# The first 640 steps of a banded-attention and feed-forward kernel, put into another explicit order

## The chip, the cores and the metric

The kernel runs on one core of a Trainium2 chip. Five engines work side by side, each through its own instruction list in order: TensorE (PE, matmuls; PEld is its weight load), VectorE (DVE), ScalarE (ACT), GpSimd (POOL) and SyncE (SP); SP, ACT and POOL also issue DMAs. The metric is the device time of one execution in microseconds, the median of three runs. [...]

## The reference

Attention with a causal window of 64 over q, k, v of shape (8, 8, 576, 64) in float32, then a feed-forward layer over the 4608 tokens of width 512:

```
scores = scale * q @ k.T                  # kept where 0 <= i - j < 64, else -1e9
attn   = softmax(scores)                  # minus the row's maximum, exp, divided by the sum
x      = (attn @ v) as (4608, 512)
h      = x @ w_in                         # (512, 2048), given as float64
out    = maximum(0.01 * h, h) @ w_out     # (2048, 512), given as float64
```

## The kernel before

The tokens are cut into 9 chunks of 512 columns. Three chunks go through an "early" feed-forward path, the other six through a later one with seven products in place of eight (line 1243 and line 1309 of the profile). Attention goes in pairs m of two query units (128 queries); each pair has two blocks b = 2m and 2m+1 of four heads. Every product is made from a high and a low float32 part (three matmuls per product), so each weight and each activation has to be split on DVE and ACT first. The float64 weights come as 32 raw tiles n (even: w_in, odd: w_out, tile f = n // 2) and are turned into float32 on DVE with integer operations.

The first stage, which this change is about, is written step by step in a string ORDER. A step's name is a kind and a number:

- attention: `S` scores of pair m on PE (64 small matmuls, L369, with two mask matmuls, L403, ahead of them but for m = 0); `Z` masks of the first pair; `E` copies a block's scores to memory (blocks 0 and 1 on DVE, L413, the others on ACT, L415); `P` the maximum over partitions on POOL (L423); `N` subtracts that maximum in PSUM by a matmul (blocks 0 to 3, L437), `sub` does so on DVE (L428, later blocks); `exp` on ACT; `V` the product with v on PE (L458); `sm`, `rec`, `y` the normalisation on DVE (L465, L470, L477); `T` a transpose on PE (L484); `H` and `L` the high part on ACT (L488) and low part on DVE (L492) of x.
- weights: `raw` the DMA of 512 KB (three buffers), `bits`, `sign`, `clamp`, `join` on DVE (L317, L321, L329, L334), `abs` on ACT between sign and clamp (L325), `chi` the high part on ACT and a DMA of the float32 tile to DRAM (`w_single`, L337 and L338), `rest` the low part on DVE (L342). `join` of tile n needs the tile that n-2 has sent off.
- feed-forward: `M` is x times w_in of job k (12 matmuls, L522), `lk`, `gh` (ACT) and `gl` (DVE, L536) the activation, `W` the product with w_out (L558). Jobs 0 to 5 are half chunks. M of job k needs the `rest` of its w_in tile and the `L` of the chunk's pairs.
- `X` with a number n is n matmuls without use (L594), `idle` in the trace.

After these 514 steps come 2303 planned operations whose order stands as numbers in a second table, PLACES (`arrange`, L442). They hold the rest of the weights, the stores of split weights, the other attention pairs and everything behind. At the end the kernel pins each engine to the order in which its instructions were written, so the tables alone set each engine's list. Nothing is reordered between engines at run time: an engine waits at the head of its list. SP's list holds the loads of q, k and v and the first three raw tiles; ACT's list holds the other raw loads.

Of the kernel before, what the change touches and what calls it, by code (L numbers as in the profile page):

```python
# [61 lines left out]
PLACES = """  # L62
# [134 lines left out]
def band_attention_ffn(ctx: ExitStack, tc: tile.TileContext, qk, vW, vL, w_in, w_out, eye_mask, out, outT):  # L197
# [415 lines left out]
    def step(name):  # L613
        kind = name.rstrip("0123456789")
        return partial(acts[kind], int(name[len(kind) :]))

    order, late = ORDER.split("|")
    for name in order.split():
        step(name)()
    prev = jobs[-1]  # L620


    plan = []

# [951 lines left out]
```

## Time and profile before

| | |
|---|---|
| median of 3 runs | 841.18 us (840.93 to 842.61) |
| span of the profiled execution | 841.2 us |
| PE busy | 829.1 us, 99% |
| DVE busy | 630.8 us, 75% |
| ACT busy | 369.7 us, 44% |
| POOL busy | 381.5 us, 45% |
| granted TensorE clock, mean | 0.998 of full |

The profiled execution's span equals the median, so sums made in the span can be set against the median directly. The first stage fills roughly the first 90 us. An engine's share of busy time is a mean over stages; in the first stage DVE is nearly as full as PE.

### The profile page before, as it was taken

What the parts mean: (1) busy time and instruction counts of PE and PEld (TensorE: products, weight loads), DVE (VectorE), ACT (ScalarE), POOL (GpSimd) and SP (SyncE); (2) the same over time, 40 slices, a digit from 0 to 9 for tenths busy, and PEclk for the clock granted to TensorE, in tenths of its full rate; (3) what the DMA queues carried; (4) which work ended last, traced back from release to release, by engine and by line L of the source; (5) the groups of instructions that cost most, each with busy time, mean ns of one, the idle gap of its engine ahead of it and who ended that gap; (6) DMA issues with size and microseconds to landing.
All of it is one profiled execution on the core that took longest, in us unless ns stands there. A gap on an engine that the chain in (4) does not pass through costs nothing.

```text
span 841.2 us, 16743 instructions
## 1 busy us (share of the span) xinstructions
PE 829.1 (99%) x6733; PEld 678.1 (81%) x6733; DVE 630.8 (75%) x912; ACT 369.7 (44%) x599; POOL 381.5 (45%) x216
## 2 busy tenths in 40 slices
PE   8999999999999999989999999999999999999997
PEld 5777888888888888868888888887888888888886
DVE  6999897777766698667888987559799863366773
ACT  4666555344423355243564442233545422325432
POOL 5332000897867747687672116797941111111110
PEclk9999999999999999999999999999999999999999
DMA  9886866987887899999999798899998996677772
GB/s 327 278 276 209 310 223 225 319 287 259 277 295 251 271 342 379 365 299 359 361 321 308 224 316 251 255 282 241 261 278 243 317 257 184 190 197 200 212 200 89
DMA packets 131005, 225.75 MB, mean 268 GB/s; under 512 B 15856, under 2 KB 53744, under 8 KB 130928
## 3 DMA queue, kind: packets, MB, share of 16 engines
q0 software_dynamic: 53568, 88.09, 38.8%
q10 hardware_dynamic: 36608, 78.26, 27.6%
q1 hardware_dynamic: 40752, 58.34, 21.7%
q8 instruction: 53, 0.87, 0.4%
q14 instruction: 24, 0.20, 0.1%
HBM read 167.28 MB, written 57.26 MB: 267 GB/s over the span
## 4 chain that ended last, share of the span: by engine, by line
PE 89%; DMA 5%; DVE 3%; issue 1%; ACT 1%; POOL 0%; DVEq 0%; ACTq 0%
PE z L1309 27%; PE m L1243 25%; PE acc L1047 11%; PE h L1038 11%; PE acc L558 4%; PE s L369 4%; PE h L522 4%; PE o L829 3%; DMA w_sums<-pspare 2%; DMA qk<-qk 1%; DMA raw<-w_in 1%; DMA raw<-w_out 1%; DMA w_single<-w 1%; PE o L458 0%; DVE raw L321 0%
## 5 line engine op out<-in xcount | busy, mean ns | idle before, releaser
L1243 PE MATMUL m<-pfew,p 128*128 128x512 f32 x720 | 171.6, 394 | 3.0 <-ACT pxa L1249 2.5
L1243 PEld LDWEIGHTS m<-pfew,p 128*128 128x128 f32 x720 | 135.5, 189 | 32.5 <-ACT pxa L1249 2.9
L1309 PE MATMUL z<-gs,p 128*128 128x512 f32 (+1 forms) x360 | 86.0, 387 | 0.0
L1047 PE MATMUL acc<-p,gs 128*128 128x512 f32 x324 | 80.7, 393 | 0.0
L1309 PE MATMUL z<-pxa,p 128*128 128x512 f32 x324 | 78.5, 391 | 0.0
L1309 PEld LDWEIGHTS z<-gs,p 128*128 128x128 f32 x360 | 67.3, 188 | 13.9
L1309 PE MATMUL z<-pspare,p 128*128 128x512 f32 x324 | 78.0, 389 | 0.0
L1252 DVE TENSOR_TENSOR pxa<-m,pxa 128x512 f32<-128x512 f32 x60 | 41.2, 688 | 48.5 <-PE m L1243 43.6
L770 POOL PARTITION_ALL_REDUCE g<-late_f x20 | 36.3, 1842 | 86.6 <-DVE late_f L755 71.5
L1227 POOL DMA_DIRECT2D p<-w_first x42 | 31.7, 755 | 93.7 <-PE m L1243 51.6
L1309 PEld LDWEIGHTS z<-pspare,p 128*128 128x128 f32 x324 | 60.7, 188 | 12.6
L1309 PEld LDWEIGHTS z<-pxa,p 128*128 128x128 f32 x324 | 60.5, 188 | 12.9 <-issue 0.2
L1243 PE MATMUL m<-pxb,p 128*128 128x512 f32 x288 | 70.6, 391 | 0.0
L1047 PEld LDWEIGHTS acc<-p,gs 128*128 128x128 f32 x324 | 60.0, 188 | 12.8
L773 POOL PARTITION_ALL_REDUCE late_o<-late_f x20 | 65.2, 3274 | 9.6 <-ACT late_f L781 7.4
L773 POOL PARTITION_ALL_REDUCE late_o<-e x18 | 61.5, 3432 | 16.6 <-issue 7.9
L1252 DVE TENSOR_TENSOR p<-m,pxa 128x512 f32<-128x512 f32 x60 | 40.7, 687 | 36.6 <-PE m L1243 35.9
L773 POOL PARTITION_ALL_REDUCE late_o<-late_e x18 | 59.3, 3321 | 10.6 <-ACT late_e L781 6.0
L1243 PEld LDWEIGHTS m<-pxb,p 128*128 128x128 f32 x288 | 53.8, 188 | 11.4
L1227 POOL DMA_DIRECT2D p<-w_sums x24 | 18.0, 749 | 93.1 <-PE z L1309 76.8
L1038 PE MATMUL h<-pxa,p 128*128 128x512 f32 x228 | 55.9, 392 | 0.0
L1038 PEld LDWEIGHTS h<-pxa,p 128*128 128x128 f32 x228 | 42.4, 188 | 9.0
(201 smaller groups left out, 1600.5 us busy)
## 6 DMA issues: line engine op xcount, KB each, us to landing
p<-w_first POOLq DMA_DIRECT2D x42, 1024.0 KB, 7.0
p<-w_sums POOLq DMA_DIRECT2D x24, 1024.0 KB, 6.7
p<-w_second POOLq DMA_DIRECT2D x18, 1024.0 KB, 6.9
qk<-qk ACTq DMA_DIRECT2D x26, 512.0 KB, 6.2
w_single<-w ACTq DMA_DIRECT2D x32, 256.0 KB, 3.7
raw<-w_out ACTq DMA_DIRECT2D x15, 512.0 KB, 4.5
raw<-w_in ACTq DMA_DIRECT2D x14, 512.0 KB, 4.3
more_v<-vL ACTq DMA_DIRECT2D x14, 512.0 KB, 6.0
```

What stands on the lines that cost most here:

```text
L369: nc.tensor.matmul(ps[j][t, c : c + QB], k[i][s, p], q[s, w, p], start=not begun and (not more or (w, p) == (0, 0)), stop=not begun and no ...
L522: nc.tensor.matmul(ps, a[:, k, :], b[:, k, part], start=n == 0, stop=n == len(terms) - 1)
L558: nc.tensor.matmul(acc[c, i], a[:, ts], b, start=begin and n == 0, stop=end and n == 2)
L770: nc.gpsimd.partition_all_reduce(most_of(j), e_of(m)[:, j], P, ReduceOp.max)
L773: nc.gpsimd.partition_all_reduce(sum_of(j), e_of(m)[:, j], P, ReduceOp.add)
L829: nc.tensor.matmul(ps[64 * j : 64 * j + 64, c : c + QB], v[:, 2 * p + j], e_of(m)[:, j, c : c + QB], start=True, stop=True,)
L1038: nc.tensor.matmul(ps, a[:, k, :], b[:, k], start=i == 0, stop=i == len(terms) - 1)
L1047: nc.tensor.matmul(acc[c, i], a[:, i * P : (i + 1) * P], b, start=begin and k == 0, stop=n in ends and k == 2)
L1227: nc.gpsimd.dma_start(to, of, max_dma_last_dim=2048)
L1243: nc.tensor.matmul(tiles[b], w[:, 256 * i + 128 * kt : 256 * i + 128 * kt + 128], x_part(OF_X[k], j, kt), start=begin and c == 0, stop=c = ...
L1252: nc.vector.tensor_tensor(to(), tiles[b], x(), ALU.add)
L1309: nc.tensor.matmul(tiles[b + i][:, cut], a, x[:, cut], start=begin and f == first and c == 0, stop=f == half - 1 and c == 2, skip_group_ch ...
```

## The change

ORDER and PLACES are merged into one table ORDER, in which names and plan numbers stand in one sequence; the steps of the last eight weight parts move to a list of their own (LATE_WEIGHTS), which only makes the plan. `arrange` walks the one table. The set of the 2817 steps is the same; from place 639 on the sequence is the same as well.

```diff
-PLACES = """
-30 1 7 40 0 38 39 5 2 31 3 10 32 17 41 42 43 44 13 33 34 4 6 45 35 36 9 51 8 12 11 14 15 52 48 16 18 23 49 53 19 59 20 149 50 22 54 21 162
...
 ORDER = """
-raw0 k1 X6 S0 q1 E1 X2 Z1 E0 bits0 sign0 Z0 P1 S1 abs0 v0 P0 raw1 clamp0 join0 N1 E3 bits1 exp1 N0 q2 P3 V1 exp0 sign1
...
+X6 q1 raw0 X2 X1 k1 X2 S0 v0 E1 E0 P1 P0 raw1 bits0 Z1 Z0 sign0 S1 k2 N1 abs0 N0 E2 q2 exp1 V1 raw2 exp0 clamp0 P2 v1 V0 S2 E3 join0 q3
...
-    order, late = ORDER.split("|")
-    for name in order.split():
-        step(name)()
...
-        for n in map(int, PLACES.split()):
+        for word in ORDER.split():
+            if not word.isdigit():
+                yield step(word)
+                continue
+            n = int(word)
...
-    for name in late.split():
+    for name in LATE_WEIGHTS.split():
```

What it moves is read from the instruction lists. Lines of the kernel after are four less than those of the kernel before.

PE's list at its start; `idle` is X, `s_0` and `s_1` the scores of the first pair. Before:

```order
1 L594 MATMUL idle_108<-p_11_93 128x512 x6
2 L369 MATMUL s_0_115<-qk_83 64x64
3 L369 MATMUL s_1_116<-qk_83 64x64
...
34 L594 MATMUL idle_151<-p_11_93 128x512 x2
35 L403 MATMUL s_1_116<-away,unit 128x512
```

and now:

```order
1 L590 MATMUL idle_107<-p_11_93 128x512 x6
2 L590 MATMUL idle_117<-p_11_93 128x512 x2
3 L590 MATMUL idle_120<-p_11_93 128x512
4 L590 MATMUL idle_123<-p_11_93 128x512 x2
5 L365 MATMUL s_0_126<-qk_83 64x64
6 L365 MATMUL s_1_127<-qk_83 64x64
```

All eleven idle matmuls stand ahead of the first scores; before, two stood behind them, one ahead of the second transpose (T1) and two ahead of the first product (M0).

PE's list a little later, around the first transpose (`t0` is T0; L437 is N, L458 is V; the number behind s and o is the pair's or the block's). Before:

```order
109 L437 MATMUL s1_0_160<-p13_2_79,p15_0_77 128x512
110 L437 MATMUL s1_1_161<-p15_0_77 128x512
111 L484 MATMUL t0_298<-unit_74,y0_291 128x128 x4
112 L458 MATMUL o2_308<-p15_0_77,p13_2_79 64x65 x8
113 L458 MATMUL o3_326<-p15_0_77,p13_2_79 64x65 x8
```

and now:

```order
111 L433 MATMUL s1_0_171<-p13_2_79,p15_0_77 128x512
112 L480 MATMUL t0_294<-unit_74,y0_291 128x128 x4
113 L433 MATMUL s1_1_172<-p15_0_77 128x512
114 L454 MATMUL o2_315<-p15_0_77,p13_2_79 64x65 x8
115 L454 MATMUL o3_327<-p15_0_77,p13_2_79 64x65 x8
```

T0 stands ahead of N3; the three still stand between N2 and V2.

DVE's list between the first and the second low part of x (`pxa1`: the first is L0; L428 is sub, L342 is rest, raw2 with L317 is bits2). Before:

```order
19 L342 TENSOR_TENSOR pfew_3_85<-w1_285,pfew_3_85 128x512
20 L317 TENSOR_SCALAR raw2_296<-raw2_296 128x512
21 L428 TENSOR_TENSOR e_76<-e_76,g_80 128x512
22 L465 TENSOR_SCALAR sm2_319<-o2_308 128x4
23 L321 SCALAR_TENSOR_TENSOR raw2_296<-raw2_296 128x512
24 L465 TENSOR_SCALAR sm3_336<-o3_326 128x4
25 L470 RECIPROCAL sm2_319<-sm2_319 128x4
26 L470 RECIPROCAL sm3_336<-sm3_336 128x4
27 L477 TENSOR_TENSOR y1_341<-o2_308,sm2_319 128x4x64
28 L492 TENSOR_TENSOR pxa1_13_324<-t0_298,pxa0_12_323 128x4x128
```

and now:

```order
19 L338 TENSOR_TENSOR pfew_3_85<-w0_275,pfew_3_85 128x512
20 L461 TENSOR_SCALAR sm2_338<-o2_315 128x4
21 L466 RECIPROCAL sm2_338<-sm2_338 128x4
22 L317 SCALAR_TENSOR_TENSOR raw2_223<-raw2_223 128x512
23 L338 TENSOR_TENSOR pfew_3_85<-w1_305,pfew_3_85 128x512
24 L461 TENSOR_SCALAR sm3_344<-o3_327 128x4
25 L424 TENSOR_TENSOR e_76<-e_76,g_80 128x512
26 L473 TENSOR_TENSOR y1_347<-o2_315,sm2_338 128x4x64
27 L466 RECIPROCAL sm3_344<-sm3_344 128x4
28 L473 TENSOR_TENSOR y1_347<-o3_327,sm3_344 128x4x64
29 L488 TENSOR_TENSOR pxa1_13_325<-t0_294,pxa0_12_324 128x4x128
```

`rest1` and `sub4` stood ahead of `sm2` and stand behind it now. What follows up to the second low part, L1, is the same set of instructions in both (`y3` stood behind L0 and stands ahead of it now).

Further on, between M0 and the sixth W, W0 goes behind S4, V9 ahead of W3, and W4, T4 and V10 ahead of M6; on DVE `y9` is ahead of rest6, bits9, sign9, clamp8, join8 and gl5, which stood ahead of it before. On SP, the load of q1 is ahead of raw0, and two stores of split weights (plan numbers 38 and 40) go out earlier. From W6 on PE's steps differ only by neighbours that change places.

## Rows read from the trace of the kernel before

**Rows 1.** The page: busy us, share of the span, instructions of each engine.
```profile
PE 829.1 (99%) x6733; PEld 678.1 (81%) x6733; DVE 630.8 (75%) x912; ACT 369.7 (44%) x599; POOL 381.5 (45%) x216
```
**Rows 2.** Busy time by stretch (us from start: length, busy and instructions, clock, DMA).
```profile
60.00:80.00 20.00, 20.00 (x189) 16.12 (x189) 19.27 (x42) 13.91 (x25) 7.88 (x4) 1.00 0.80 251
24.53:59.94 35.41, 34.27 (x439) 28.14 (x439) 32.90 (x77) 22.58 (x45) 12.11 (x6) 1.00 0.85 272
```
**Rows 3.** Waits of PE over the whole span (total us, times, longest).
```profile
PE m L1243 <- ACT pxa L1249: 2.5, 1, 2.5
PE t L484 <- DVE y L477: 1.4, 2, 0.7
```
**Rows 4.** Timeline, PE's start (start us, us, instructions, idle before).
```profile
1.45 2.93 PE L594 MATMUL idle<-p 128*128 128x512 f32 x6 [1.45 <-DVE p L605]
4.60 1.61 PE L369 MATMUL s<-qk 64*64 64x64 f32 x64 [0.22 <-DMA qk<-qk]
```
**Rows 5.** The idle matmuls alone (duration ns min/median/max, first and last start).
```profile
L594 PE MATMUL idle<-p x11: 397/628/793, 1.4 to 24.0; 128*128 128x512 f32 x11
```
**Rows 6.** The first scores alone by stretch of 0.2 us (PE, PEld, clock, DMA).
```profile
5.20:5.40 0.20, 0.20 (x17) 0.20 (x15) 1.00 1.04 430
...
5.80:6.00 0.20, 0.20 (x29) 0.20 (x20) 1.00 0.78 277
```
**Rows 7.** Timeline: from E of the first pair to S2.
```profile
6.29 1.29 DVE L413 SCALAR_TENSOR_TENSOR e<-s,p 128x512 f32<-128x512 f32 x2 [4.90 <-PE s L369]
...
11.10 1.12 PE L437 MATMUL s<-g,p 128*128 128x512 f32 x2 [0.22 <-POOL g L423]
...
11.26 1.09 DVE L317 TENSOR_SCALAR raw<-raw 128x512 uint32<-128x512 uint32 x1 [0.16 <-DMA raw<-w_out]
...
13.52 0.73 PE L403 MATMUL s<-away,unit 128*128 128x512 f32 x2
```
**Rows 8.** Timeline: from N2 to M0.
```profile
15.48 1.13 PE L437 MATMUL s<-p,p 128*128 128x512 f32 x2
...
16.65 1.08 DVE L342 TENSOR_TENSOR pfew<-w,pfew 128x512 fp32r<-128x512 f32 x1
...
17.83 1.15 PE L458 MATMUL o<-p,p 128*64 128x65 f32 x32
...
18.13 0.67 DVE L428 TENSOR_TENSOR e<-e,g 128x512 f32<-128x512 f32 x1
...
18.73 0.15 DVE L465 TENSOR_SCALAR sm<-o 128x4 f32<-128x4 f32 x1
...
18.92 0.73 PE L403 MATMUL s<-away,unit 128*128 128x512 f32 x2
...
19.58 1.16 PE L369 MATMUL s<-p 64*64 64x64 f32 x64
...
20.67 0.50 PE L594 MATMUL idle<-p 128*128 128x512 f32 x1
...
21.87 0.63 PE L484 MATMUL t<-unit,y 128*128 128x128 f32 x4 [0.69 <-DVE y L477]
...
23.65 0.73 PE L594 MATMUL idle<-p 128*128 128x512 f32 x2
...
23.91 0.68 DVE L492 TENSOR_TENSOR pxa<-t,pxa 128x512 fp32r<-128x512 f32 x1
...
24.53 1.68 PE L522 MATMUL h<-pxa,pfew 128*128 128x256 f32 x12
```
**Rows 9.** Timeline: bits7, join8 and T4.
```profile
39.53 0.43 DVE L317 TENSOR_SCALAR raw<-raw 128x512 uint32<-128x512 uint32 x1 [1.33 <-DMA raw<-w_out]
...
49.51 0.69 DVE L334 SCALAR_TENSOR_TENSOR w<-raw 128x512 uint32<-128x512 uint32 x1 [0.88 <-DMA w_single<-w]
...
52.14 0.63 PE L484 MATMUL t<-unit,y 128*128 128x128 f32 x4 [0.73 <-DVE y L477]
```
**Rows 10.** The chain that ended last, one piece (start us, us, what).
```profile
343.71 14.64 DMA w_sums<-pspare
```

More of the change, by code (lines that the diff above doesn't have):

```diff
@@ L60 @@
 )
-PLACES = """
[77 rows of a table removed]
-"""
-ORDER = """
-raw0 k1 X6 S0 q1 E1 X2 Z1 E0 bits0 sign0 Z0 P1 S1 abs0 v0 P0 raw1 clamp0 join0 N1 E3 bits1 exp1 N0 q2 P3 V1 exp0 sign1
-V0 k2 E2 P2 sm0 rec0 S2 sm1 abs1 rec1 chi0 E4 clamp1 N2 q4 rest0 v1 join1 q3 chi1 exp2 y1 y0 rest1 N3 raw2 T0 bits2
-exp3 P4 k3 sub4 V2 raw3 sm2 E5 sign2 H0 V3 abs2 sm3 rec2 P5 rec3 y2 L0 exp4 v2 clamp2 y3 sub5 join2 raw4 S3 X1 T1
-bits3 exp5 H1 V4 E6 V5 chi2 P6 sm4 v3 sign3 L1 sm5 rec4 X2 M0 rec5 y4 k5 y5 rest2 k4 E7 abs3 raw5 clamp3 lk0 bits4
@@ L146 @@
-join3 gh0 T2 gl0 H2 sub6 sign4 L2 abs4 M1 P7 W0 clamp4 exp6 join4 raw6 lk1 v4 S4 sub7 V6 bits5 chi4 exp7 rest4 sm6
-sign5 E8 V7 sm7 rec6 rec7 gh1 y6 chi3 q6 P8 abs5 y7 M2 raw7 gl1 T3 rest3 E9 q5 H3 W1 sub8 lk2 clamp5 exp8 L3 bits6 gh2
-join5 P9 raw8 gl2 chi5 V8 bits7 M3 sign6 rest5 lk3 abs6 gh3 S5 sign7 abs7 M4 clamp6 q7 v5 gl3 W2 join6 lk4 raw9 sub9
-clamp7 M5 bits8 exp9 join7 sign8 gh4 sm8 W3 rec8 E10 y8 chi6 P10 abs8 gl4 clamp8 chi7 rest6 raw10 lk5 sub10 V9 join8
-bits9 gh5 exp10 W4 v6 sm9 sign9 k6 rec9 gl5 M6 y9 T4 V10 chi8 rest8 abs9 raw11 lk6 rest7 bits10 clamp9 M7 gh6 H4 sm10
@@ L151 @@
-sign10 E11 join9 W5 abs10 chi9 rec10 L4 y10 clamp10 bits11 join10 P11 sub11 S6 gl6 raw12 rest9 exp11 sign11 chi10 V11
-E12 raw13 rest10 abs11 lk7 sm11 gh7 rec11 P12 y11 W6 E13 T5 clamp11 bits12 join11 sign12 abs12 H5 raw14 gl7 bits13 k7
-sub12 clamp12 exp12 L5 join12 sign13 M8 chi11 chi12 W7 lk8 P13 rest11 raw15 rest12 sub13 bits14 abs13 S7 clamp13 V12
-sign14 join13 sm12 exp13 rec12 y12 E14 gh8 q9 abs14 M9 gl8 clamp14 v7 V13 W8 P14 raw16 bits15 sub14 join14 sm13 rec13
-lk9 y13 E15 chi14 exp14 chi13 rest14 sign15 T6 rest13 raw17 V14 gh9 P15 sm14 sub15 abs15 clamp15 H6 M10 rec14 gl9
@@ L156 @@
-exp15 y14 k8 join15 L6 bits16 V15 W9 sm15 lk10 sign16 raw18 rec15 chi15 rest15 gh10 y15 T7 gl10 abs16 H7 clamp16
-join16 W10 bits17 L7 M11 raw19 sign17 M12 bits18 abs17 chi16 ev0 clamp17 join17 sign18 raw20 bits19 abs18 lk11 chi17
-sign19 rest16 gh11 clamp18 join18 v8 gl11 bits20 chi18 rest17 raw21 ev1 sign20 lk12 rest18 abs19 clamp19 join19 bits21
-gh12 gl12 M13 W11 raw22 abs20 M14 chi19 lk13 sign21 clamp20 abs21 gh13 W12 join20 gl13 clamp21 raw23 lk14 bits22
-sign22 rest19 chi20 gh14 rest20 M15 W13 abs22 join21 bits23 clamp22 raw24 chi21 sign23 join22 chi22 gl14 M16 raw25 W14
@@ L161 @@
-abs23 rest21 bits24 sign24 lk15 clamp23 abs24 join23 gh15 rest22 gl15 bits25 clamp24 M17 sign25 chi23 raw26 lk16 gh16
-abs25 W15 join24 gl16 M18 chi24 clamp25 raw27 rest23 q8 bits26 sign26 abs26 lk17 join25 chi25 rest24 gh17 clamp26
-join26 gl17 bits27 sign27 raw28 abs27 chi26 W16 rest25 lk18 clamp27 join27 rest26 chi27 gh18 bits28 sign28 gl18 W17
-|
+ORDER = """
+X6 q1 raw0 X2 X1 k1 X2 S0 v0 E1 E0 P1 P0 raw1 bits0 Z1 Z0 sign0 S1 k2 N1 abs0 N0 E2 q2 exp1 V1 raw2 exp0 clamp0 P2 v1 V0 S2 E3 join0 q3
@@ new lines @@
+bits1 sign1 sm0 abs1 sm1 chi0 rec1 N2 rec0 P3 y1 y0 T0 E4 clamp1 N3 bits2 exp2 exp3 join1 k3 raw3 rest0 raw4 chi1 V2 H0 V3 v2 P4 sm2 rec2
+sign2 rest1 abs2 sm3 sub4 y2 rec3 y3 E5 v3 L0 exp4 S3 clamp2 V4 P5 T1 H1 join2 sub5 exp5 E6 V5 P6 bits3 sm4 sign3 L1 sm5 chi2 abs3 k4 rec4
+y4 k5 M0 rec5 y5 rest2 bits4 sign4 T2 E7 q4 raw5 lk0 sub6 gh0 M1 H2 exp6 abs4 clamp3 L2 P7 gl0 lk1 join3 gh1 V6 q5 raw6 clamp4 S4 join4 W0
+sub7 chi4 exp7 bits5 rest4 E8 v4 sign5 raw7 abs5 sm6 V7 rec6 M2 sm7 chi3 rec7 E9 P8 y6 y7 gl1 rest3 sub8 clamp5 T3 H3 L3 exp8 bits6 W1
@@ new lines @@
+join5 sign6 raw8 bits7 V8 M3 chi5 rest5 q6 v5 sign7 lk2 lk3 abs6 S5 clamp6 gh2 M4 k6 gh3 P9 sub9 exp9 gl2 sm8 E10 gl3 lk4 join6 abs7 rec8
+W2 gh4 y8 bits8 clamp7 V9 raw9 chi6 join7 gl4 P10 sm9 W3 M5 raw10 E11 rec9 sub10 sign8 y9 chi7 abs8 lk5 P11 W4 exp10 rest6 bits9 sign9 T4
+rest7 H4 clamp8 V10 join8 M6 gh5 chi8 L4 raw11 gl5 sub11 abs9 lk6 clamp9 sm10 join9 exp11 gh6 bits10 sign10 rec10 raw12 abs10 W5 S6 rest8
+gl6 clamp10 y10 M7 join10 chi9 chi10 raw13 E12 lk7 V11 rest9 bits11 sign11 P12 sm11 rec11 y11 bits12 abs11 clamp11 rest10 k7 v6 sign12 E13
@@ new lines @@
+abs12 join11 W6 T5 clamp12 sub12 join12 raw14 H5 exp12 L5 bits13 sign13 raw15 q7 M8 gh7 chi11 chi12 P13 gl7 V12 sub13 S7 sm12 W7 rest12
+rest11 rec12 E14 y12 lk8 bits14 P14 gh8 bits15 exp13 gl8 sign14 abs13 V13 clamp13 abs14 join13 raw16 M9 clamp14 join14 chi14 sm13 chi13 v7
+W8 rec13 E15 sign15 sub14 y13 raw17 exp14 P15 rest14 V14 lk9 gh9 rest13 abs15 sm14 40 bits16 sub15 clamp15 T6 M10 rec14 v8 y14 H6 exp15
+join15 gl9 V15 38 raw18 lk10 q8 W9 sign16 sm15 chi15 L6 rec15 y15 bits17 gh10 T7 gl10 abs16 rest15 H7 W10 clamp16 sign17 join16 abs17
@@ new lines @@
+bits18 chi16 clamp17 L7 ev0 raw19 M11 join17 chi17 sign18 ev1 lk11 abs18 rest16 rest17 gh11 clamp18 M12 gl11 bits19 raw20 join18 lk12
+chi18 gh12 sign19 gl12 abs19 clamp19 join19 M13 raw21 bits20 W11 lk13 sign20 M14 chi19 rest18 gh13 abs20 raw22 gl13 W12 clamp20 join20
+bits21 sign21 raw23 chi20 rest19 abs21 lk14 M15 clamp21 join21 gh14 rest20 bits22 chi21 W13 M16 sign22 bits23 gl14 raw24 abs22 lk15
+clamp22 join22 sign23 raw25 abs23 chi22 gh15 clamp23 rest21 gl15 join23 bits24 lk16 sign24 abs24 rest22 raw26 W14 clamp24 join24 gh16
@@ L165 @@
+raw27 bits25 sign25 gl16 M17 bits26 M18 sign26 W15 chi23 q9 chi24 lk17 abs25 rest23 abs26 clamp25 30 bits27 k8 sign27 join25 raw28 clamp26
+abs27 gh17 clamp27 rest24 chi25 join26 31 gl17 rest25 1 lk18 bits28 41 W16 join27 chi26 W17 gh18 gl18 5 rest26 sign28 chi27 0 4 6 8 2 3 11
[77 rows of a table added]
+"""
+LATE_WEIGHTS = """
 abs28 raw29 clamp28 join28 bits29 raw30 sign29 rest27 abs29 bits30 chi28 clamp29 sign30 rest28 abs30 join29 clamp30
@@ L615, in step @@
         return partial(acts[kind], int(name[len(kind) :]))
-    order, late = ORDER.split("|")
-    for name in order.split():
-        step(name)()
     prev = jobs[-1]
+    turns_late = counter(len(jobs))
     plan = []
@@ L735, in band_attention_ffn @@
         }[kind]
-        more = [weights_of.get(n - 2, {}).get("rest")] if kind == "join" else []
-        o[kind] = op(engine, us, step(name), *(o.get(b) for b in before), *more, rank=0.3)
+        room_of = [weights_of.get(n - 2, {}).get("rest")] if kind == "join" else []
+        o[kind] = op(engine, us, step(name), *(o.get(b) for b in before), *room_of, rank=0.3)
     all_in = [weights_of[n][k] for n in (28, 29, 30, 31) for k in ("join", "rest")] + [weights_of[27]["rest"]]
@@ L1024, in band_attention_ffn @@
     ends = {n for n in range(len(walk)) if n + 1 == len(walk) or walk[n][0] != walk[n + 1][0]}
-    pair_at = [pairs_of_g[next(turns) % 2] for _ in walk]
+    pair_at = [pairs_of_g[next(turns_late) % 2] for _ in walk]
     h_of, tiles, stage = {}, {}, {}
```

153 rows, old and new, of tables (ORDER, PLACES) are left out of this document.

## The prediction

> **What bounds the kernel now.** I read the page first: PE is busy 829.1 of 841.2 us, 99% [rows 1]. The same matmuls run before and after, so the time can move only by what PE waits, or by matmuls that run below full pace. The table of PE's waits comes second: one wait of 2.5 us far behind the first stage, and two of 0.7 us for `y`, the normalised block that a transpose reads [rows 3]. Third, busy time by stretch: from M0 at 24.53 to W6 at 59.94, 35.41 us, PE is busy 34.27, so 1.14 us are idle; from 60 to 80 it is busy all the time [rows 2]. So the first 60 us decide, and there DVE is nearly as full as PE: 32.90 of the 35.41 us, and 19.27 of the 20 after that [rows 2]. Fourth, the timeline of those 60 us, to see which DVE result PE needs next. In it S0, the first scores, waits for its DMA until 4.60 [rows 4]; from there a chain of E, the maximum on POOL, N, exp and V leads to S2 at 13.52 [rows 7]; M0 starts at 24.53, just as the low part L1 ends on DVE (23.91 plus 0.68) [rows 8].
>
> **The idle matmuls at the start.** Six stand ahead of S0 now, eleven after. [...] The seventh idle matmul would start at 1.45 + 6 x 0.43 = 4.03, the tenth at 5.32, the eleventh at about 5.66, and S0 at about 5.9, all its data being there since 4.60. S0 then runs at full pace: 1.16 us, as S3's scores do [rows 8], in place of 1.61 [rows 4]. It ends at 7.06, E starts 0.08 later (4.60 + 1.61 = 6.21 against 6.29 in the trace [rows 4, 7]), at 7.14 instead of 6.29: +0.85. Bounds: +0.1 if the pace doubles as the first six end (then the other five take half of 0.43 each: 4.03 + 1.08 + 1.16 + 0.08 = 6.35), +1.7 if nothing is at full pace before S0 ends (4.03 + 2.15 + 1.61 + 0.08 = 7.9, less 6.29). I take +0.85, since the second half of S0 shows the doubling itself.
>
> Two idle matmuls behind S0 cost nothing before, since PE waited there for E. That wait hides no more and no less afterwards.
>
> **From E to M0.** E, two POOL maxima, N0 (11.10, released by POOL), exp and V0 follow one on another, with no slack in it, so S2 starts at 13.52 + 0.85 = 14.37. The two maxima P2 and P3 change places on POOL, to the order in which N2 and N3 want them; S2 no longer ends on a wait for P2. I give S2 the length of S3, 20.67 - 18.92 = 1.75 [rows 8]. N2, N3 and T0 took 17.83 - 15.48 = 2.35 in either order; from V2 to `sm2` it was 18.73 - 17.83 = 0.90 [rows 8]. So `sm2` can start at 14.37 + 1.75 + 2.35 + 0.90 = 19.37 instead of 18.73: +0.64.
>
> On DVE, `rest1` and `sub4` were done before `sm2` (16.65 and 18.13 [rows 8]); after, they stand behind it. DVE stands and waits for `sm2` instead: from S2's start to `sm2` it was 18.73 - 13.52 = 5.21, less 1.08 and 0.60 for these two it is 3.5, so DVE is there at 14.37 + 3.5 = 17.9, some 1.4 us early. From `sm2` to the end of L1 it took 23.91 + 0.68 - 18.73 = 5.86 us of unbroken work. To this come `rest1` and `sub4`, 0.60 each at the pace at which DVE issues such tiles (18.73 - 18.13): 7.06. L1 ends at 26.43 instead of 24.59: +1.84. M0 cannot go past its first matmul without L1, so M0 goes from 24.53 to about 26.35: +1.8. The idle matmuls that are gone from this place (at 20.67 and 23.65) and the wait of 0.69 ahead of T1 [rows 8] give nothing back, because PE would only wait for L1 in their stead. Bounds of this shift: 0.85 - 1.15 - 0.69 = -1.0 if PE alone decided (three idle matmuls fewer behind `sm2`'s chain and two behind S0, at about 0.23, and no wait for T1), and +2.5 if a DVE tile meets POOL on the way at the price below.
>
> POOL's share: bits1 took 1.09 us while a maximum ran, and 0.43 elsewhere [rows 7, 9], so one meeting costs DVE up to 0.66. There are sixteen maxima in both versions. Which tile meets which changes; in sum I count nothing, and +-0.6 in the range. [...]
>
> **From M0 to W6.** PE does the same matmuls between these two points, in a better order: W4, T4 and V10 come ahead of M6, and `y9`, for which T4 stood 0.73 us [rows 9], comes on DVE ahead of six tiles that it stood behind. These are rest6, join8 and sign9 at 0.60, clamp8, bits9 and gl5 at about 0.35: 2.9 us. Also gone from its path is the wait of join8 for a DMA, 0.88 [rows 9]. So with L1 1.84 late, y9 is still about 1.9 earlier than it was. T4 stood at 52.14; with M6 (12 matmuls of full width, 2.6 at half of 0.43 each) behind it now, it must come 2.6 earlier than 52.14 to keep the end, and with an end 0.66 later 1.9 earlier: tight, but without a loss. The other 0.4 us (1.14 less 0.73) are short waits; there PE comes later than before while DVE has lost its two waits for DMAs [rows 9], so it finds its tiles ready. I take back all of the 1.14 us of idle [rows 2], and no more, since no idle is left after that. Bounds: 0 to 1.14.
>
> **The rest.** From 60 us to 80 PE has no idle [rows 2], and behind W6 neighbours change places with the same sums. The two stores that go earlier on SP lie in a time when their tiles are ready; cost nothing, or a load of v or q delayed by one transfer, none of which PE waits for there. The stall of 2.5 us later on [rows 3] comes from a transfer of w_sums that takes 14.64 us from its issue [rows 10]. The issue hangs on PE's own progress and moves with it, so I carry the shift through.
>
> **Sum.** +1.8 at M0, -1.14 up to W6: +0.66. The profiled span, 841.2, is the median of the runs as well, so 841.9 us. A measurement of this kernel can tell about 0.2%, 1.7 us, from no change; this lies within it.
>
> **Rivals.**
> 1. PE decides and not DVE: M0 comes 1.0 earlier (the lower bound above), the 1.14 are saved as well, -2.1: 839.1. For it: DVE waits some 1.4 us ahead of `sm2`, room in which a different pace of V2 would put `rest1`; the five idle matmuls really are gone from the middle. Against it: every instruction between `sm2` and L1 is needed or stands in the queue, and L1 ended when M0 began.
> 2. Slower: DVE decides up to W6. DVE is at 93% there [rows 2]; its two waits, 1.33 for raw7 and 0.88 for the tile that join8 replaces [rows 9], are waits for DMAs that were themselves issued behind a `join`. If these land 1.8 later with all else, the room they gave is not there, and each PE step behind M0 waits for its tile as before: the whole +1.8 stays, and a meeting with POOL in L1's path adds 0.66: +2.5, 843.7; without the meeting 843.0. It decides from the point at which raw7 or raw8 lands after DVE gets to its bits. For it: the DMA engines are at 85% in the stretch [rows 2]. Against: raw7 stands ahead of abs5 on ACT now, so it is issued sooner after its buffer is free.
> 3. The transfer of 14.64 us lands earlier or later against PE after any shift: without the stall the kernel takes 841.9 - 2.5 = 839.4, with one as much longer 844.4. For: its time is queueing; against: what is queued there moves with PE.
> [...]
> 5. The order does nothing: what is lost at the start is exactly found again, 841.2. It ends where the forecast does, within 1.7 us.
>
> **How the numbers follow.** Forecast and rival 5 together 0.42, all of it within 0.2%. Rival 1 0.24, of which 0.19 beyond 1.7 us. Rival 2 0.22, of which 0.19 beyond. Rival 3 0.09: faster 0.04, slower 0.05. Rival 4 0.03, slower. That gives faster 0.23, slower 0.27, and 0.50 within. The range leaves out the outer part of rivals 1 and 3 below and of 2 and 3 above: 838.9 to 843.8. The forecast's own range is 841.0 to 842.8: 0.3 to 0.5 for the clock's rise and 0.6 for POOL.
>
> **What would show it.** In the profile after: eleven idle matmuls from 1.45, ending near 5.9, and the first E near 7.1; a wait of DVE of 1 to 1.5 us ahead of `sm2` near 19.4; L1 ending and M0 starting near 26.4; no wait of PE ahead of T4; W6 near 60.6 and PE without idle from there. If M0 starts before 24.5, rival 1 holds; if M0 is near 26.4 and W6 beyond 61.5, rival 2; if W6 is where I put it and the end is not, look at the stall near 360 us. The forecast is wrong if the first scores start before 5.4, or if L1 ends with DVE idle ahead of it.

## The result, and the profile after

The kernel after takes 849.36 us (median of 4 runs, 847.72 to 849.75), the kernel before 841.89 us (4 runs, 840.93 to 843.77): a ratio of 1.0090, 95% interval 1.0068 to 1.0112. It is slower by some 7.5 us, outside the range I gave. The profiled execution has a span of 847.9 us (its time is 849.7, so 1.8 us lie around the span), 6.7 more than the 841.2 of before. In all runs that have both on record the time is 1.7 to 1.9 us longer than the span, so the profiled execution of before took some 843.0 us itself (an estimate from its span). That its span equals the median is chance; below, spans are set against spans only.

The page's busy line, stretches of it (60 to 80, and M0 to W6, now 29.16 to 66.24), and PE's waits over the whole span, of the kernel after. They answer to [rows 1 to 3]:

```profile
PE 830.6 (98%) x6733; PEld 677.6 (80%) x6733; DVE 636.7 (75%) x912; ACT 369.3 (44%) x599; POOL 378.9 (45%) x216
```
```profile
60.00:80.00 20.00, 19.49 (x241) 14.91 (x240) 19.55 (x41) 12.09 (x22) 6.36 (x3) 1.00 0.82 267
29.16:66.24 37.08, 34.74 (x442) 28.16 (x438) 34.70 (x77) 23.04 (x46) 11.54 (x6) 1.00 0.77 233
```
```profile
PE o L454 <- ACT e L440: 3.1, 3, 2.2
PE s L365 <- DMA qk<-qk: 2.6, 2, 1.6
PE h L518 <- ACT g L523: 2.0, 1, 2.0
...
PE h L518 <- DVE pxb L488: 1.0, 1, 1.0
```

M0 to W6 takes 37.08 us instead of 35.41, with 2.34 us of idle instead of 1.14. Two of the waits are ones that the kernel before did not have at all: a product `h` for ScalarE's `g` (2.0), and a product `h` for `pxb`, the low part L7 (1.0). Two others have grown: V for exp (3.1, longest 2.2) and scores for a load (2.6). The long wait of before, `m` for `pxa` [rows 3], is gone.

The start, as the chain of waits shows it (start, us, what), and the first scores by stretches of 0.2 us, against [rows 4, 6]:

```profile
1.45 2.94 PE idle L590 x6
...
4.43 1.24 PE idle L590 x2
...
5.71 0.81 PE idle L590
...
6.57 1.22 PE idle L590 x2
7.79 1.96 PE s L365 x64
...
9.77 0.70 DVE e L409
```
```profile
8.20:8.40 0.20, 0.20 (x18) 1.00 1.04 405
...
9.00:9.20 0.20, 0.20 (x20) 1.00 1.20 474
```

The four groups of idle matmuls do not follow at one pace: each starts 0.04 to 0.05 us behind the end of the one before (4.39 to 4.43, 5.67 to 5.71, 6.52 to 6.57), and its weight load waits 0.56 to 0.78 for that end. A group of one takes 0.81 and a group of two 1.24, where one matmul in the middle of a group takes 0.43. And the first scores stay at 20 matmuls a slice at most, the slow pace, to their end; in before the pace rose from 17 to 29 within them [rows 6]. E starts at 9.77 instead of 6.29.

Then M0, in the timeline (start, us, engine, line, instruction, idle before), against [rows 8]:

```profile
21.86 0.16 DVE L461 TENSOR_SCALAR sm<-o 128x4 f32<-128x4 f32 x1 [0.50 <-PE o L454]
...
27.14 0.69 DVE L424 TENSOR_TENSOR e<-e,g 128x512 f32<-128x512 f32 x1
...
27.86 0.63 ACT L440 ACTIVATE e<-e 128x512 f32<-128x512 f32 x1 [0.87 <-DVE e L424]
...
28.55 0.69 PE L454 MATMUL o<-v,e 128*64 128x65 f32 x16 [2.18 <-ACT e L440]
...
28.81 0.69 DVE L488 TENSOR_TENSOR pxa<-t,pxa 128x512 fp32r<-128x512 f32 x1
...
29.16 1.98 PE L518 MATMUL h<-pxa,pfew 128*128 128x256 f32 x12
```

L1 ends at 29.50 and M0 starts at 29.16, 4.63 later than before. PE waits 2.18 for exp5 (27.86) ahead of it: sub5 (27.14) stands behind clamp2 and join2 on DVE now.

Next come M3, T4 and the first product of the late path, M11. In the kernel before, lk2 (35.65) was done long before M3 (37.23), and M11 (88.17) ran without a wait:

```profile
35.65 0.39 ACT L527 ACTIVATE g<-h 128x256 f32<-128x256 f32 x1
...
37.23 1.70 PE L522 MATMUL h<-pxa,pfew 128*128 128x256 f32 x12
...
88.17 8.32 PE L522 MATMUL h<-pxb,pfew 128*128 128x512 f32 x36
```

In the timeline of after, chi5 is the CAST at 43.49 and lk2 the ACTIVATE behind it, clamp6 stands at 47.18, and L7 is the `pxb` at 95.99:

```profile
42.41 0.68 DVE L330 SCALAR_TENSOR_TENSOR w<-raw 128x512 uint32<-128x512 uint32 x1
...
43.49 0.62 ACT L333 CAST pfew<-w 128x512 fp32r<-128x512 f32 x1 [1.86 <-DVE w L330]
...
44.02 0.38 ACT L523 ACTIVATE g<-h 128x256 f32<-128x256 f32 x1
...
44.45 1.69 PE L518 MATMUL h<-pxa,pfew 128*128 128x256 f32 x12 [1.97 <-ACT g L523]
...
47.18 0.43 DVE L325 TENSOR_SCALAR raw<-raw 128x512 f32<-128x512 f32 x1 [1.73 <-ACT raw L321]
...
55.57 0.60 PE L480 MATMUL t<-unit,y 128*128 128x128 f32 x4
...
95.31 0.43 DVE L313 TENSOR_SCALAR raw<-raw 128x512 uint32<-128x512 uint32 x1 [1.15 <-DMA raw<-w_in]
...
95.99 0.68 DVE L488 TENSOR_TENSOR pxb<-t,pxb 128x512 fp32r<-128x512 f32 x1
...
96.73 2.57 PE L518 MATMUL h<-pxb,pfew 128*128 128x512 f32 x10 [1.05 <-DVE pxb L488]
```

M3 needs the bank that lk2 reads. lk2 stood ahead of exp8 and stands behind chi5 now, chi5 waits for join5, and so PE waits 1.97 us for an ACT instruction of 0.38. From there it goes round to DVE: lk3 and abs6 stand behind lk2 on ACT, lk3 has to wait for M3, and clamp6 on DVE waits 1.73 us for abs6, a wait that before did not have. At M11, L7 stands behind bits18, which waits for its raw tile; before, L7 stood ahead of it. T4 has no wait any more [rows 9]. The transfer of w_sums in the chain is there still, shorter than in [rows 10], and a load of q and k behind it; no product `m` waits for the two now, only the scores, at 372.83:

```profile
354.02 11.31 DMA w_sums<-pspare
...
365.40 7.29 DMA qk<-qk
...
372.83 1.28 PE s L365 x64
```

**An account.** Three things give nearly the whole span: the time at which M11 runs through (88.17 before, 96.73 after, where its first matmul is done when the wait for L7 comes), the idle time of PE behind 100 us, and what the granted clock loses there. What is left is 747.5 to 748.5 us in twelve profiles of fourteen, 748.1 after and 747.9 before (the other two have 748.6 and 749.3). To get the idle time and the clock's loss I add 5 less busy, and 5 x (1 - granted clock), over stretches of 5 us from 100 to 835.

| order | M0 | M11 runs through | M0 to M11 | idle and slow clock behind 100 us | span |
|---|---|---|---|---|---|
| before | 24.53 | 88.17 | 63.6 | 5.1 | 841.2 |
| after | 29.16 | 96.73 | 67.6 | 3.1 | 847.9 |
| old front, new rest (experiment 5) | 25.84 | 94.38 | 68.5 | 5.5 | 847.5 |
| the same, L7 early (10) | 24.60 | 92.23 | 67.6 | 1.2 | 841.3 |
| the same, lk2 and L7 early (7) | 25.36 | 89.80 | 64.4 | 2.2 | 839.5 |
| before, lk2 late (11) | 24.38 | 90.58 | 66.2 | 0.8 | 839.1 |
| new front, old rest (6) | 27.91 | 91.90 | 64.0 | 2.2 | 841.9 |
| after, lk2 and L7 early (9) | 27.00 | 91.33 | 64.3 | 4.4 | 843.4 |

So after's +6.7 is +8.6 at M11 and 2.0 given back behind it. The 8.6 are 4.6 up to M0, 1.7 from there to W6 (37.08 less 35.41), and 2.3 from W6 to M11 (96.73 - 66.24 = 30.49, less 88.17 - 59.94 = 28.23).

Each row is one execution. The times of one order differ by 2 to 8 us, so the place of M11 says more on the order than one span does. M0 differs between executions too: five profiles with the same order up to M0 (before, 5, 7, 10 and 11) have it at 24.38 to 25.84, and three with the new front (after, 6 and 9) at 27.00 to 29.16. So 1.3 to 2.2 us of after's 4.6 belong to its execution, and what the order behind M0 costs is read from M0 to M11. That takes 3.9 to 4.9 us more than in before with the new rest, 0.7 to 0.8 more once lk2 and L7 are put forward in it, whichever front stands ahead, and 0.4 more with the old rest.

### The profile page after: what moved, and what is told of

The parts are those of the page before. It is cut to its first block, busy times and chain, and to the rows that moved or that the text cites. A ratio compares the mean times of both kernels' runs of the same rounds, so it can differ in the third digit from the quotient of the medians.

```text
span 847.9 us, 16737 instructions
## 1 busy us (share of the span) xinstructions
PE 830.6 (98%) x6733; PEld 677.6 (80%) x6733; DVE 636.7 (75%) x912; ACT 369.3 (44%) x599; POOL 378.9 (45%) x216
## 4 chain that ended last, share of the span: by engine, by line
PE 83%; DVE 7%; DMA 5%; issue 2%; POOL 1%; ACT 1%; ACTq 0%; SPq 0%; POOLq 0%; DVEq 0%
PE z L1307 27%; PE m L1241 25%; PE acc L1045 9%; PE h L1036 9%; PE s L365 4%; PE h L518 3%; PE o L827 3%; PE acc L554 2%; DMA qk<-qk 1%; DMA w_sums<-pspare 1%; DVE w L330 1%; DVE raw L317 1%; DMA raw<-w_in 1%; PE idle L590 1%; DVE p L338 1%
## 5 line engine op out<-in xcount | busy, mean ns | idle before, releaser
L1241 PE MATMUL m<-pfew,p 128*128 128x512 f32 x720 | 169.7, 391 | 0.5 <-DVE pxa L1250 0.5
L771 POOL PARTITION_ALL_REDUCE late_o<-late_e x18 | 59.0, 3303 | 15.3 <-ACT late_e L779 11.1
```

Of the source, the lines that this page charges most:

```text
L771: nc.gpsimd.partition_all_reduce(sum_of(j), e_of(m)[:, j], P, ReduceOp.add)
L1241: nc.tensor.matmul(tiles[b], w[:, 256 * i + 128 * kt : 256 * i + 128 * kt + 128], x_part(OF_X[k], j, kt), start=begin and c == 0, stop=c = ...
```

## Experiments

All are edits of the sequence; the rest is the text of after. Each was timed together with before: before has 839.36 us beside the first four, 839.70 beside the next four and 839.88 beside the last four, which ran on another chip. After was not timed again, so ratios to before are compared; after's is 1.0090 (1.0068 to 1.0112).

**1. The idle matmuls at their old places** (edit against after):

```diff
-X6 q1 raw0 X2 X1 k1 X2 S0 v0
+X6 q1 raw0 k1 S0 X2 v0
...
-V4 P5 T1
+V4 P5 X1 T1
...
-k5 M0
+k5 X2 M0
```


> The kernel after, with the five idle matmuls put back where the kernel before had them (two behind S0, one ahead of T1, two ahead of M0); all else as after. Theory A (each group of idle matmuls waits until the one before it has drained, so S0 starts at 7.72 in place of 4.60 and is all at the slow pace): S0 at 4.6, first E at 6.3 in place of 9.77, M0 and W6 about 3.3 earlier than after, time 845.5 to 846.5. Rival B (the new order on DVE and ACT costs the time, the start is swallowed by waits on DVE): E at 6.3, but M0 at 28 or later and the time 848.5 to 849.5.

847.37 us, ratio 1.0093 (1.0069 to 1.0116). S0 starts at 4.50 and E at 6.03, so the start is mended, and sm2 at 19.00, but M0 is at 28.12, M3 at 44.29 (after 44.45), and the end no better (after's ratio is 1.0090). The wait for exp5 is there (2.08 us), and behind it the granted clock falls to 0.50 (columns as in [rows 2]):

```profile
24.00:26.00 2.00, 0.22 (x4) 0.22 (x6) 2.00 (x5) 1.23 (x3) 0.00 (x0) 0.91 1.06 396
26.00:28.00 2.00, 2.00 (x18) 1.23 (x16) 1.70 (x7) 1.77 (x4) 1.70 (x1) 0.50 1.01 379
```

In this order the earlier start brings no earlier end: what is gained is lost again by M3. From M0 to M3 it takes 16.2 us and in after 15.3, since the clock stays at 0.50 up to 32.

**2. All eleven as one group** (against after):

```diff
-X6 q1 raw0 X2 X1 k1 X2 S0
+X11 q1 raw0 k1 S0
```


> The kernel after, with all eleven idle matmuls as one group (X11) in place of X6 X2 X1 X2: the same eleven matmuls, no draining between groups. Theory A: they come every 0.43 us at most, S0 starts at 5.9 to 6.2 and the first E at 7.1 to 7.9, 2 to 2.6 earlier than after; time 846.8 to 847.6. Rival A2 (the number of slow matmuls costs, not the draining): S0 at 7.4 or later, time within 1 of after, 848.5 to 849.5.

849.44 us, ratio 1.0115 (1.0092 to 1.0137). PE's start in the timeline:

```profile
1.45 4.32 PE L581 MATMUL idle<-p 128*128 128x512 f32 x11 [1.45 <-DVE p L592]
5.69 1.16 PE L356 MATMUL s<-qk 64*64 64x64 f32 x64
```

With no break between groups S0 is at 5.69 and E at 6.92, 0.63 behind before: near the +0.85 of the forecast. The groups add 0.8 to 1.2 (E at 7.67 to 8.14 in experiments 9, 3 and 6), and what is left of after's +3.48 is the slow pace of its groups and scores up to 9.7: against experiment 9 the groups behind the sixth matmul take 1.27 more and the scores 0.82. The end is again no better.

**3. Before, with its idle matmuls in front** (against before; X1 and X2 further on go):

```diff
-raw0 k1 X6 S0 q1 E1 X2 Z1
+raw0 k1 X6 X2 X1 X2 S0 q1 E1 Z1
```


> The kernel before, with its later five idle matmuls moved to the front as X6 X2 X1 X2; this part of the change alone. Theory A: first E at 9.8, M0 near 27.9, W6 near 63, time 3 to 3.5 over before, 844.9 to 845.6. Rival B: the middle has 1.15 us of idle matmuls fewer and the waits there shrink, time at most 1 over before.

841.77 us, ratio 1.0034 (1.0017 to 1.0052): slower by 2.4 to 2.9 us. E is at 7.81 (+1.52), M0 at 25.17 (its second matmul waits for L1 until 26.16), M11 at 89.38 (+1.2). With the old order behind it, most of the late start stays.

**4. The first, with lk2 ahead of exp8** (against experiment 1):

```diff
-L3 exp8 bits6 W1 join5 sign6 raw8 bits7 V8 M3 chi5 rest5 q6 v5 sign7 lk2 lk3
+L3 lk2 exp8 bits6 W1 join5 sign6 raw8 bits7 V8 M3 chi5 rest5 q6 v5 sign7 lk3
```


> As e1, and lk2 put ahead of exp8 on ACT as in the kernel before (after has it behind chi5). Theory A+C (M3 waits 1.97 for lk2, since M3's bank is the one that lk2 reads, and lk2 stands behind chi5, which waits for join5): no wait of M3 for ACT g, W6 and the end 1.5 to 2 earlier than e1: about 844. Rival D (another wait for a DVE tile takes its place): within 0.7 of e1.

846.38 us, ratio 1.0082 (1.0057 to 1.0107). M3 has no wait for ACT and is 2.8 us earlier (41.47), 0.9 of which lie at M2 already (37.23 against 38.15). M11 runs through at 93.88 instead of 96.45, still after a wait for L7 (1.11). The median moved by 1 us only, which the intervals do not tell apart from nothing: this profile has 4.7 us of idle behind 100 us, experiment 1 has 1.9.

**5. Before's order up to M0, after's behind it** (the joint):

```diff
-sm5 chi2 abs3 k4 rec4 y4 k5 M0 rec5 y5
+sm5 rec4 X2 M0 abs3 k4 y4 k5 rec5 y5
```


> The order of before up to and with the first product M0, then what is left in the order of after. Theory A (the two parts of the new order cost on their own: about 4.6 us up to M0 and about 2 to 3.5 us behind it, less the 2.5 us stall near 360 us that is gone): M0 at 24.5, the wait of M3 for ScalarE's lk2 (2.0 us) and that of the first late product for the low part L7 (1.1 us) stay, first h<-pxb at 90 to 91, time 841 to 842 where before has 840. Theory B (the later piece is good by itself, only the late M0 spoils it): M0 at 24.5, the first h<-pxb at or before 88.2, time 837 to 839.

848.4 us, ratio 1.0094 (1.0070 to 1.0118). Both theories priced this too low: the order behind M0 alone makes the kernel as slow as the whole change. M3 waits 2.03 us for lk2 and its 12 matmuls take 2.89 us, with the clock at 0.74 from 40 to 42 and at 0.50 from 42 to 44; clamp6 on DVE then waits 2.95 us for abs6; M11 runs through at 94.38, after 0.92 for L7.

**6. After's order up to M0, before's behind it:**

```diff
-k5 M0 rec5 y5 rest2 bits4 sign4 T2 E7 q4 raw5 lk0
+k5 M0 q4 rec5 y5 rest2 E7 raw5 clamp3 lk0 bits4 join3
```


> The order of after up to and with M0, then what is left in the order of before. Theory A: M0 near 29.2 (+4.6), no wait of M3 for lk2, the first h<-pxb 4 to 5 us later than in before (92.2 to 93.2), time 843.5 to 845 where before has 840. Rival (slack behind M0 takes the lost time back, and the whole loss comes from the later piece): M0 near 29.2, the first h<-pxb back at 88 to 89.5, time 840 to 841.5.

843.26 us, ratio 1.0044 (1.0021 to 1.0067). M0 at 27.91, M11 at 91.90 (+3.7), no wait for lk2. V5 waits 2.17 us for exp5, and the clock is at 0.50 from 26 to 32. The front costs 3 to 4 us by itself and is not found again, as theory A said.

**7. Experiment 5 with lk2 and L7 put forward** (lk2 as in experiment 4, and):

```diff
-sign17 join16 abs17 bits18 chi16 clamp17 L7 ev0
+sign17 join16 abs17 L7 bits18 chi16 clamp17 ev0
```


> As the one with before's order up to M0 and after's behind it, and two single steps put forward: lk2 ahead of exp8 on ScalarE, L7 ahead of bits18 on VectorE. Theory A: neither wait is left; M3 about 2 us, the first h<-pxb 2 to 3 us earlier than without the two edits, so at about 88; time 838 to 839.5 where before has 840. Rival (the products behind M3 wait for VectorE's tiles anyway): M3 earlier but the first h<-pxb and the time as without the two edits, within 0.5 us.

842.46 us, ratio 1.0038 (1.0020 to 1.0055). M3 and M11 in the timeline:

```profile
38.72 1.69 PE L509 MATMUL h<-pxa,pfew 128*128 128x256 f32 x12
...
89.80 8.32 PE L509 MATMUL h<-pxb,pfew 128*128 128x512 f32 x36
```

Both waits are gone, and so is clamp6's. M11 is 4.6 us earlier than in experiment 5 (4.1 from M0 on), and the median is 5.9 lower. Theory A had the direction; it put M11 at 88 and the time 3 us too low. Two steps out of the 640 carry most of what the new order costs behind M0. What makes this order still slower than before was not tried.

**8. Experiment 1 with block 5 earlier** (against experiment 1):

```diff
-S3 clamp2 V4 P5 X1 T1 H1 join2 sub5 exp5 E6 V5
+S3 P5 sub5 clamp2 V4 X1 T1 exp5 H1 join2 E6 V5
```


> After's order with the idle matmuls at before's places (as in the first experiment), and sub5 ahead of clamp2 on VectorE and exp5 ahead of H1 on ScalarE, as they stand in before. Theory A (in the first experiment V5 waited 2.08 us for exp5, which stood behind clamp2, join2 and H1, and the clock fell behind that wait): exp5 at about 23.5 instead of 25.1, V5's wait at most 0.6 us, granted clock 1.00 from 26 to 34, M0 near 26.7 (L1's end) instead of 28.1, M3 1 to 2 us earlier than 44.29; time 1 to 2 us below the first experiment's 847.4. Rival (VectorE's sum of work sets M1 and M3 whatever the order within it): M0 earlier, M3 at 44 to 44.5 and the time as in the first experiment.

849.2 us, ratio 1.0113 (1.0084 to 1.0142). V5 and M0 in the timeline, and the clock:

```profile
25.25 0.69 PE L445 MATMUL o<-v,e 128*64 128x65 f32 x16 [1.19 <-ACT e L431]
25.87 0.73 PE L581 MATMUL idle<-p 128*128 128x512 f32 x2
26.75 0.35 PE L509 MATMUL h<-pxa,pfew 128*128 128x256 f32 x1
```
```profile
26.00:28.00 2.00, 1.64 (x8) 1.03 (x9) 1.93 (x8) 1.83 (x4) 1.74 (x1) 1.00 1.03 380
```

M0 and the clock are where theory A put them, though V5 still waits 1.19 us where it said 0.6 at most. But M3 still waits 2.0 us for lk2 (42.21), now with the clock falling behind it (0.50 from 44 to 46), and M11 runs through at 95.20, 1.25 earlier only. The time did not fall; the rival's outcome, though not for its reason.

**9. After with lk2 and L7 put forward** (both edits as above):

> After's order with two single steps put forward: lk2 ahead of exp8 on ScalarE, L7 ahead of bits18 on VectorE. With before's order up to M0 the same two edits brought the time from 848.4 to 842.5. Theory A (the late front is worth 3 to 4 us to the end once these waits do not hide it, as it was with the old order behind it): M3 without wait, at about 41.7 to 42.5, the first h<-pxb at 92 to 93 with no wait behind it, time 845 to 847. Rival (the front is found again in the new rest; the two waits alone are the loss): time 842 to 844, as with the old front.

847.34 us, ratio 1.0086 (1.0062 to 1.0110). M3 and M11 in the timeline:

```profile
40.28 1.69 PE L509 MATMUL h<-pxa,pfew 128*128 128x256 f32 x12
...
91.33 6.06 PE L509 MATMUL h<-pxb,pfew 128*128 128x512 f32 x26
```

M11 comes 5.4 us earlier than in after, with no wait. Of these 2.2 lie at M0 already (27.00 against 29.16), where the order is the same, and 3.2 from M0 on. M11 is 3.2 us behind before, about as far as with the front alone (3.7, experiment 6). Neither wait is left, as theory A said, with M3 1.4 and M11 0.7 earlier than its bounds. The median does not show it: its profiled execution is the fastest of six (845.17), and even this one loses 4.4 us behind 100 us, 1.8 of them in a wait for a load of q and k that ends at 166.69, and 1.7 by the lower clock behind it (0.83 from 165 to 175).

**10. Experiment 5 with L7 put forward alone:**

> Before's order up to M0, after's behind it, and only L7 put ahead of bits18. Theory A (lk2's wait is the larger part: 2.0 us, and 1 to 2 us more when the granted clock falls behind it; L7's is 0.9): M3 still waits 2.0 us for ScalarE, the first h<-pxb has no wait behind it, time 846.5 to 848, about 1 us below the 848.4 without the edit. Rival (L7 and what follows it is the larger part): time 843 to 845.

844.65 us, ratio 1.0055 (1.0034 to 1.0075). M3 waits 2.0 us, M11 runs through at 92.23. The median is 3.7 below experiment 5, but M11 came only 2.1 earlier, 1.2 of which lie at M0 already; the profile of 5 lost 5.5 us behind 100 us, this one 1.2. So L7's own price is about its wait, 0.9 us. The time is the rival's (843 to 845), but not by L7: the places are theory A's.

**11. Before with lk2 behind chi5** (against before; gh2 and gl2, which need lk2's result, go with it):

```diff
-sub8 lk2 clamp5 exp8 L3 bits6 gh2 join5 P9 raw8 gl2 chi5 V8
+sub8 clamp5 exp8 L3 bits6 join5 P9 raw8 chi5 lk2 gh2 gl2 V8
```


> Before's order with lk2, gh2 and gl2 put directly behind chi5; PE's and VectorE's lists are those of before. In before lk2 was done at about 36.0 and chi5 began at 38.28. Theory A: M3 now waits for lk2, starts at 38.5 to 39.0 instead of 37.23, and the first h<-pxb and the end come 1 to 2 us later (841 to 842 where before has 839.7), more where the clock falls behind the wait. Rival (M4 and M5 wait for VectorE's tiles anyway, the loss is found again): M3 late, the first h<-pxb within 0.5 us of before's 88.2 and the time within 0.2%.

843.76 us, ratio 1.0046 (1.0022 to 1.0071). PE's and DVE's lists are those of before; lk2 is the ACTIVATE:

```profile
38.00 0.62 ACT L324 CAST pfew<-w 128x512 fp32r<-128x512 f32 x1 [1.86 <-DVE w L321]
...
38.52 0.38 ACT L514 ACTIVATE g<-h 128x256 f32<-128x256 f32 x1
...
38.95 2.60 PE L509 MATMUL h<-pxa,pfew 128*128 128x256 f32 x12 [1.98 <-ACT g L514]
...
39.37 0.43 DVE L523 TENSOR_TENSOR gs<-g,gs 128x256 fp32r<-128x256 f32 x1 [1.78 <-ACT gs L519]
```
```profile
38.00:40.00 2.00, 1.05 (x6) 1.05 (x7) 0.63 (x2) 1.31 (x3) 0.00 (x0) 0.84 0.70 80
40.00:42.00 2.00, 2.00 (x10) 1.69 (x8) 1.94 (x4) 0.41 (x2) 0.00 (x0) 0.50 0.79 313
```

M3 waits 1.98 us, then runs with the clock falling to 0.50. M3 is 1.7 late (38.95 against 37.23), M4 3.2 (43.61 against 40.42), M11 2.4. gl2 on DVE waits 1.78 us as well, but bits7 behind it starts at 39.71 instead of 39.53, because in before DVE waited for raw7 there [rows 9]; so little of the loss can come by that way. This one piece of the change, put alone into the old order, makes the kernel measurably slower, by 3.9 us in the median, where theory A had 1 to 2 and more if the clock fell. The only other single piece tried alone in the old order is the idle matmuls (experiment 3).

**12. All four mended** (experiment 8, with lk2 and L7 put forward):

> After's order with the idle matmuls at before's places, sub5 ahead of clamp2 and exp5 ahead of H1, lk2 ahead of exp8 and L7 ahead of bits18. Theory A (the loss is the sum of the late start, block 5's wait, lk2's and L7's): M0 at 26.7, M3 near 40 without wait for ScalarE, the first h<-pxb at 90 to 91.5 without wait behind it, time 842 to 844, near the 842.5 of the old front with the two late edits. Rival (VectorE's larger sum of work ahead of M0 costs 2 us more to the end whatever the waits): first h<-pxb at 92 to 94, time 845 to 847.

844.92 us, ratio 1.0070 (1.0047 to 1.0092). M0 26.66, M3 40.44, M11 at 92.92 without a wait behind it. The time lies just between theory and rival; M11 is the rival's. M0 is 2.1 later than in before, as in experiment 8, and its second matmul waits for L1 until 27.23. So M1 is 2.6 later (29.28 against 26.69): by that much DVE's order ahead of L1 costs, with the start mended and V5's wait down to 1.19. M11 is 4.8 later. Against experiment 7, with the same order behind M0, 1.3 us lie at M0 and 1.2 between M4 and M5. There PE waits 0.42 for a tile `gs` of DVE and 0.43 for ACT, behind a wait of DVE for raw7, which experiments 7 and 9 do not have:

```profile
43.25 0.43 DVE L304 TENSOR_SCALAR raw<-raw 128x512 uint32<-128x512 uint32 x1 [1.54 <-DMA raw<-w_out]
```

Why raw7 lands late here was not tried.

None of these orders is faster than before.

## Why the prediction was wrong

- **The idle matmuls at the start**: the direction was right, the size was not. Forecast E +0.85, bound +1.7 (its own terms give 7.87 - 6.29, so +1.6), measured +3.48. I let the groups follow back to back; in after each starts only 0.04 to 0.05 us behind the end of the one before, whose last matmul takes up to 0.80 by itself. The 0.43 us a matmul in the terms is (2.93 - 0.79) / 5 [rows 4, 5] and holds in after too, and the rise of the pace within S0 is that from 17 to 29 matmuls a slice [rows 6]. No run with this start shows the 5.9 for S0: in the timelines it is at 7.72 in after, at the slow pace to its end, and at 6.45 to 6.91 in experiments 9, 3 and 6. The forecast for one group is borne out by experiment 2 (+0.63). With the groups, E came at 7.67 (experiment 9), 7.81 (3) and 8.14 (6), so 1.4 to 1.9 late; the 3.48 of the profile after has the slow pace up to 9.7 besides.
- **From E to sm2**: forecast 0.21 shorter than before, measured 0.35 (3.13 late at sm2, 3.48 at E). Right. DVE waited 0.50 for it, not 1 to 1.5.
- **From sm2 to L1**: forecast 7.06, measured 29.50 - 21.86 = 7.64. Near it, and M0 gets past its first matmul only as L1 ends. I did not see that sub5 goes behind join2 and that V5 then waits 2.18 for exp5. In after V5 ends just ahead of L1, so this cost next to nothing there; where the clock fell behind it, it did (experiment 6: M0 to M1 3.4 us, in before 2.2).
- **From M0 to W6**: this is the step that failed. I wrote that PE "comes later than before while DVE has lost its two waits for DMAs [rows 9], so it finds its tiles ready" and took back 1.14. DVE did lose both waits, but PE lost 1.67 instead. I followed DVE's list alone, as if DVE waited for DMAs only. The wait that replaced the others is for ACT: lk2 stands behind chi5, and PE waits 2.0 us for it at M3. By lk3 and abs6 the same step makes DVE wait 1.73. So y9, which I had put about 1.9 us earlier than before, came 2.6 later (54.17 against 51.58); T4 went without a wait because PE was late itself. Experiment 11 shows lk2's price alone, experiment 7 shows the loss gone with it and L7.
- **The rest**: I put it at nothing, "neighbours change places with the same sums". One of these neighbours is L7, behind a tile that waits for its DMA: 1.05 at M11. W6 to M11 took 2.3 longer; 1.55 of it is PE idle, with 0.4 for a `y` of DVE beside L7's wait.
- **Rivals.** Rival 2 had the right sign. Its mechanism, raw7 and raw8 landing late, did not occur in after: the waits of DVE in [rows 9] are gone. It did in experiment 12, with 1.54 for raw7. Rival 3's stall of 2.5 is gone, with 1.0 for a load of q and k in its place and 1.6 for another at 171.81; behind 100 us PE lost 3.1 in place of 5.1, which hid 2.0 of the loss. Rivals 1 and 5 fell. No run shows a term behind the 0.03 of rival 4. What after shows of DVE tiles beside a maximum is 1.33 us for bits1 (the maximum 2.07) and 1.52 for rest0 (1.91), where such tiles take 0.42 and 0.68. That is 0.91 and 0.84 more, above my price of 0.66. DVE still waited for a product of V behind each (0.58 and 0.50), so they cost this path nothing.

**What is shown and what is open.** Shown, in the first 100 us: the front by itself brings M11 3.7 us late (experiment 6, the slow clock behind V5 included), lk2 by itself 2.4 (11), L7 about its wait, 0.9 (5 against 10). With lk2 and L7 mended, M0 to M11 takes 3.2 us less than in after (9) and 4.1 less than in experiment 5 (7). The three prices make 7.0 of after's 8.6 at M11; its M0 is 1.3 later than that of experiment 6, which has the same order up to there. Since M0 alone differs by 1.5 to 2.2 us between executions of one order, this sum is no better than that. Open: what PE loses behind 100 us. It ran from 0.8 to 5.5 us in the profiles, and the ratios of experiments 5 and 9 (1.0094 and 1.0086) are as high as after's although M11 came earlier than in after. So the medians alone do not show the whole 7.5 us as the sum of these pieces. A wait of 0.7 to 1.8 us for a load of q and k between 165 and 172 us stands in five of the ten profiles with the new order behind M0 (after, 4, 5, 7 and 9), in none with the old; which transfer ahead of it decides was not tried.

## What to carry to other kernels

Of a new order, read every engine's list, the one with slack too. An instruction of 0.38 us that frees a buffer held up the fullest engine for 1.97 us here, once it was put behind a step that waits for another engine (lk2 behind chi5). For each instruction that TensorE waits for, ask what stands ahead of it on its own engine and what that waits for. When ends scatter, look for a late milestone behind which the time is constant but for idle time and clock. Compare the orders there, and see first how far one order's own milestones scatter.

## What the runs showed of the hardware

- The groups of idle matmuls, each into a new tile of the same buffer, do not follow back to back: in after each starts 0.04 to 0.05 us behind the end of the one before. At the slow pace a group of two took 1.24 us and one of one 0.81, where one more within a group takes 0.43; at the full pace it was 0.73 and 0.52 (experiment 9).
- The pace of the first matmuls rose at about 5.6 us in before, from 17 in a slice of 0.2 us to 29 [rows 6]; in after the scores never came above 20 a slice up to their end at 9.7, with a granted clock of 1.00 in all these rows. In experiment 9, with the same start as after, the second group took 0.75 already:

```profile
4.43 0.75 PE idle L581 x2
...
5.22 0.52 PE idle L581
...
5.78 0.73 PE idle L581 x2
6.52 1.14 PE s L356 x64
```

  Each kernel here has one trace; the four with this start (after, 3, 6 and 9) have E at 9.77, 7.81, 8.14 and 7.67. What sets the time at which the pace rises was not shown.
- A wait of PE of about 2 us was followed by a granted clock of 0.50 in some profiles and not in others: behind M3's wait for lk2 (1.97 to 2.03) in four profiles of seven (5, 8, 10 and 11, not after, 1 and 2), behind V5's wait for exp5 (2.08 to 2.18) in four of six (1, 2, 4 and 6, not after and 9). Where it fell at M3, M4 came 4.7 us behind M3 instead of 3.2: 1.5 us more than the wait.
